# Order within a slot of a fused attention and expert kernel: short products, 1/l and lower parts moved, x's split in quarters

## The chip, the cores and the metric

The kernel runs on one core of one Trainium2 chip. Its engines are TensorE (PE, with its weight loads PEld), VectorE (DVE), ScalarE (ACT), GpSimd (POOL) and SyncE (SP), which only issues transfers here. The metric is the device time of one execution in microseconds (us).

## The reference

Attention with a compressive memory (4 batches, 8 heads, 576 positions, 64 dimensions), and behind it an expert layer over all 2304 tokens:

```python
scores = scale * np.matmul(q, k.transpose(0, 1, 3, 2))        # causal mask
a = np.exp(scores - scores.max(-1, keepdims=True))
a /= a.sum(-1, keepdims=True) + 1e-09
local = np.matmul(a, v)
mem_out = np.einsum('bhsd,bhde->bhse', phi(q), M_prev) / mem_norm
x = g * mem_out + (1 - g) * local                             # g: gate from beta
h = x @ w_in                                                  # 512 -> 2048
out = softplus(h) @ w_out                                     # 2048 -> 512
```

Inputs are wide; the kernel keeps nearly full single precision with products of two parts, an upper and a lower one (high x high, high x low, low x high).

## The kernel before

**Units and slots.** The first part of the program is the attention. A unit is two heads of one batch, 16 units in all. A unit has four slots: slot 0 does the query chunks 0 and 1 of 128 rows, slot 1 chunk 2, slot 2 chunk 3, slot 3 the last half chunk; 64 slots in all, and three more at the end for what is late. In this text units count from 1, slots of a unit from 0, and slots of the whole loop (t in the code) from 0.

**The work of a slot.** `emit_S`: scores on PE into `s` (two buffers), the maximum `nm` on DVE (L357, or L376 in slot 3), `nm` scaled on ACT, and P with its row sums l on ACT (L364, L378). One slot later `emit_split`: r = 1/l on DVE (`rr`, L390 and L393), then the upper half of P times r on POOL (L408, L417) and the lower half on DVE (L409, L419), both into `PHL`; SP's transposing transfers bring them into `PTA` or `PTB`. Three slots after its scores comes `emit_pv`: it turns the memory's part `mem` into the PSUM tile `xp` (L433) and adds P times v (L443); ACT copies the result into `x` (L446). The first part of a unit (A, 256 positions) has its `emit_pv` in slot 3, the second (B, 320 positions) in slot 2 of the next unit.

**Preparation.** For the next unit small steps lie in fixed slots: in slot 2 `v0b` makes v's scale `sc` on DVE from the short PE product `sp`; in slot 3 `f2` makes `ph` (ACT, then DVE, L305); in slot 0 `v2` makes v's lower half; in slot 1 `f3` has the products `np` on PE (L314) and from them `mem` on DVE (L315 to L318, eight operations). `np` uses the PSUM buffers `sm` and `xp`, so the next `emit_pv` comes behind `mem` on PE.

**Expert pieces.** As soon as tokens are complete, four blocks of 384 tokens get a first share of the expert layer while the attention still runs: a piece a slot, six of 12 matmuls (`hp`, one for each of six groups of 128 expert columns, L153) and then four of 18 (`op`, L153). `fill_step` issues a piece; what follows it on other engines (`posts`: Softplus and cast on ACT, the lower part of g on DVE, L91; for `op` the copy `pb` and its transfer) comes in the next slot. Before a block's first piece `split_x` splits x into upper parts (POOL, L99) and lower ones (DVE, L91), four of each. The weights arrive as 64-bit floats; a decode step takes one POOL, three DVE operations (L137 to L141), a cast on ACT and a subtraction on DVE (L91), 12 steps at `WRATE` a slot.

**What sets the order.** In the attention part PE, DVE, ACT and POOL run in the order in which the code issues (a manual schedule); SP's queue is ordered by a scheduler. A slot is issued as: `posts`; `emit_S`; `emit_split` of the slot before; `emit_pv`; the piece; the preparation steps; a decode. After the attention the rest of the expert layer runs under the scheduler, which may also put pieces of it into the last slots.

Of the kernel before, what the change touches and what calls it, by code (L numbers as in the profile page):

```python
# [11 lines left out]
F32R = mybir.dt.float32r  # L12
# [17 lines left out]
GRPS = [6, 10]  # L30
NWB = 6
PVLAG = 3
WRATE = 0.6
GA = GRPS[0]


# [10 lines left out]
def attn_softplus_moe(  # L47
# [28 lines left out]
    x = res.tile([128, NP, NT], F32, name="x")  # L76
# [6 lines left out]
    CAP = 384  # L83
# [6 lines left out]
    def sub(eng, out, in0, in1):  # L90
        eng.tensor_tensor(out=out, in0=in0, in1=in1, op=ALU.subtract)  # L91
# [80 lines left out]
    def emit_g(pool, hp, n, cap, gb):  # L172
        l = pool.tile([128, cap], F32, tag="l", name="l", bufs=3)[:, :n]
        g = pool.tile([128, 2, cap], F32R, tag="g", name="g", bufs=gb)
        A.activation(out=l, in_=hp[:, :n], func=AF.Softplus)  # L175
        cast(A, g[:, 0, :n], l)
        sub(V, g[:, 1, :n], l, g[:, 0, :n])
        return g

    def out_pairs(f, g, dm, n):  # L180
        w = wt[f]
        wh, wl = w[:, 1, 0, dm * 128:(dm + 1) * 128], w[:, 1, 1, dm * 128:(dm + 1) * 128]
        return [(wh, g[:, 0, :n]), (wh, g[:, 1, :n]), (wl, g[:, 0, :n])]

    blocks, work, ready, posts = deque(), deque(), {}, deque()
    XLAG = 2

    def split_x(pool, t0, kd, xt, ea, eb):
        src = x[:, kd, t0:t0 + CAP]
# [3 lines left out]
    def push_fill(k):  # L193
        st = {}
        t0 = k * CAP

        def xs():
            st["x"] = moe1.tile([128, 2, 4, CAP], F32R, tag="xhl", name="xhl", bufs=1)
            for kd in range(4):
                split_x(moe1, t0, kd, st["x"], P, V)  # L200

        def h(f):
            hp = emit_h(moe1, f, st["x"], CAP, CAP)

            def post():
                st[f] = emit_g(moe1, hp, CAP, CAP, GA)
            return post

        def o(dm):
            op = ps_r.tile([128, 512], F32, tag="h", name="op", bufs=2)  # L210
            pairs = []
            for f in range(GA):
                pairs += out_pairs(f, st[f], dm, CAP)
            mm3(op[:, :CAP], pairs, True, True)

            def post():
                pb = moe1.tile([128, CAP], F32, tag="l", name="pb", bufs=3)
                A.copy(pb, op[:, :CAP])
                SY.dma_start(out=part[:, dm, t0:t0 + CAP], in_=pb)
            return post  # L220

        blocks.append((k, xs))
        work.extend([(12, k, h, f) for f in range(GA)] + [(3 * GA, k, o, dm) for dm in range(4)])

    def next_block(t):
        if blocks:
            k, xs = blocks.popleft()
            xs()
            done.add(k)
            ready[k] = t + XLAG  # L230

    def fill_step(t, force=False):

        if not work:
            return
        n, k, fn, j = work[0]
        if k not in done:
            next_block(t)  # L240
        if not force and ready.get(k, 1 << 30) > t:
            return
        work.popleft()
        posts.append(fn(j))
        if n == 12 and j == GA - 1:
            next_block(t)

    def run_posts():
        while posts:
            posts.popleft()()  # L250


    units = [Unit(b, p) for b in range(B) for p in range(NP)]
# [126 lines left out]
            w = 1  # L380
        return pts, l[:, :w]

    def emit_split(u, cs, pts, l):
        r = at.tile([128, 4], F32, tag="rr", name="rr", bufs=3)[:, :l.shape[1]]
        p = u.p
        if cs == (4,):
            ci = cinv4[:, p:p + 1]
        else:
            ci = cinv[:, 2 * p:2 * p + 2].unsqueeze(1).to_broadcast([128, len(cs), 2])
        V.scalar_tensor_tensor(out=r if cs == (4,) else r.rearrange("p (c h) -> p c h", h=2),  # L390
                               in0=l if cs == (4,) else l.rearrange("p (c h) -> p c h", h=2),
                               scalar=1e-9 * ESH, in1=ci, op0=ALU.add, op1=ALU.mult)
        V.reciprocal(out=r, in_=r)  # L393
        w = "A" if cs[0] < 2 else "B"
        if w not in u.pt:
            shape = [128, 8, 256] if w == "A" else [128, 18, 320]
            u.pt[w] = at.tile(shape, F16, tag="PT" + w, name="PT" + w, bufs=2 if w == "B" else 1)
        dst = u.pt[w]
        for j, c in enumerate(cs):
            pt = pts[j]  # L400
            ph = at.tile([128, (c + 1) * 512 if c < 4 else 2 * S], F16, tag=f"PHL{c}", name="PHL", bufs=1)
            if c < 4:
                nk = c + 1
                o = ph.rearrange("p (k t h s) -> p k t h s", t=2, h=2, s=128)
                for h in range(2):
                    rh = r[:, 2 * j + h:2 * j + h + 1]
                    src = pt[:, h * nk * 128:(h + 1) * nk * 128].rearrange("p (k s) -> p k s", s=128)
                    P.tensor_scalar(out=o[:, :, 0, h, :], in0=src, scalar1=rh, scalar2=0.0, op0=ALU.mult, op1=ALU.add)  # L408
                    V.scalar_tensor_tensor(out=o[:, :, 1, h, :], in0=src, scalar=rh, in1=o[:, :, 0, h, :],  # L409
                                           op0=ALU.mult, op1=ALU.subtract)  # L410
                q0 = (c - (0 if w == "A" else 2)) * 128
                SY.dma_start_transpose(out=dst[:, 0:4 * nk, q0:q0 + 128], in_=ph)
            else:
                o = ph[:, 0:1024].rearrange("p (k t s) -> p k t s", t=2, s=128)
                src = pt[:, 0:512].rearrange("p (k s) -> p k s", s=128)
                o4, s4 = ph[:, 1024:1152], pt[:, 512:576]
                P.tensor_scalar(out=o[:, :, 0, :], in0=src, scalar1=r, scalar2=0.0, op0=ALU.mult, op1=ALU.add)  # L417
                P.tensor_scalar(out=o4[:, 0:64], in0=s4, scalar1=r, scalar2=0.0, op0=ALU.mult, op1=ALU.add)
                V.scalar_tensor_tensor(out=o[:, :, 1, :], in0=src, scalar=r, in1=o[:, :, 0, :], op0=ALU.mult,  # L419
                                       op1=ALU.subtract)  # L420
                V.scalar_tensor_tensor(out=o4[:, 64:128], in0=s4, scalar=r, in1=o4[:, 0:64], op0=ALU.mult,
                                       op1=ALU.subtract)
                d = dst.rearrange("p (j h) q -> p j h q", h=2)
                for h in range(2):
                    SY.dma_start_transpose(out=d[:, :, h, 256:320], in_=ph[64 * h:64 * h + 64, 0:1152])
# [51 lines left out]
    with ExitStack():  # L477
# [26 lines left out]
        prev = None  # L504
        wcred = 0.0
        decode = deque()
        t = 0
        while t < ns or late or prev is not None:
            cur = None
            if t < ns:  # L510
                i, c = slots[t]
                u = units[i]
                if c[0] == 0 and i + 1 < len(units):
                    loads(i + 1)
                    plan(i + 1, t)
                run_posts()
                cur = (u, c) + emit_S(u, c)
                if c[0] in (0, 4):
                    late.setdefault(t + PVLAG, []).append((u, "A" if c[0] == 0 else "B"))
            else:  # L520
                run_posts()
            if prev is not None:
                emit_split(*prev)
            for a in late.pop(t, []):
                emit_pv(*a)
            fill_step(t)
            for f in prep.pop(t, []):
                f()
            if decode:
                a, b = decode.popleft()  # L530
                a()
                posts.append(b)
            wcred += WRATE
            while wcred >= 1 and pieces:
                wcred -= 1
                decode.append(pieces.popleft()())
            prev = cur
            t += 1
        run_posts()
        assert not pieces and not prep and not decode  # L540

        order.close()
        attn_ctx.close()
        while work and work[0][1] in done:
            fill_step(t, True)
            run_posts()
        wb = ctx.enter_context(tc.tile_pool(name="wb", bufs=1, side="right", reuse_waits="tile"))
        hcnt.append(0)
        moe2 = ctx.enter_context(tc.tile_pool(name="moe2", bufs=1, reuse_waits="tile"))
# [33 lines left out]
        for i in range(len(seq) + LAG):  # L583
            if i < len(seq):
                s, f = seq[i]
                fl = steps[s][2]
                fi = f - fl[0]
                hp = emit_h(moe2, f, xh[s], CAP, CAP)
                gs[i] = emit_g(moe1, hp, CAP, CAP, GA)
                for _ in range(2 if i % 3 == 0 else 1):  # L590
                    if pieces:
                        pieces.popleft()()
                if fi == 0:
                    if s == len(rest):
                        partial(s)
                    if s + 1 < len(steps):
                        partial(s + 1)
                if s + 1 < len(steps) and 1 <= fi < 5:
                    next_x(s + 1, fi - 1)
# [81 lines left out]
```

## Time and profile before

| | us |
|---|---|
| median of 3 runs | 722.59 (721.75 to 723.76) |
| profiled execution | 720.95 |
| its span, first to last instruction | 719.2 |
| attention part, until about | 410 |

| engine | busy us of the span | share |
|---|---|---|
| PE | 599.6 | 83% |
| DVE | 413.5 | 57% |
| ACT | 313.8 | 44% |
| POOL | 125.9 | 18% |

The shares are means over two parts that differ: after about 410 us PE is the one busy engine, before it PE and DVE take turns. So the rows below are cut by stretches and by slots. Times in a row are the start and the duration; the bracket at a row's end is the idle time of the engine just before it and what ended that.

### The profile page before, as it was taken

Reading aid. Unit: us, or ns where it says so; the run is one execution under the profiler, and the core shown is the slowest. Engines: PE = TensorE matmul, PEld = TensorE weight load, DVE = VectorE, ACT = ScalarE, POOL = GpSimd, SP = SyncE. Lnnn points to the kernel's source line nnn. Section 1 sums busy time; section 2 is a strip of 40 time slices with the busy share of each in tenths; the row PEclk is TensorE's granted clock in tenths of the full one; section 3 lists DMA queues with packets and bytes.
Section 4 is the critical chain, followed back from the end, with each engine's and each line's share of the span. In section 5 each row is a group of like instructions: output and inputs, shape, how many; then the busy total and the mean of one; then the engine's idle time right before and its main releaser. Section 6 shows DMA issues by size and latency. Waiting matters only on the chain.

```text
span 719.2 us, 10758 instructions
## 1 busy us (share of the span) xinstructions
PE 599.6 (83%) x3928; PEld 527.3 (73%) x3928; DVE 413.5 (57%) x918; ACT 313.8 (44%) x797; POOL 125.9 (18%) x218
## 2 busy tenths in 40 slices
PE   6553553847986679989888999999999999999998
PEld 4332332636864557767666899999999999999997
DVE  4788787887578785777678368886203122220211
ACT  6444544357565564665466245444213232321221
POOL 1323223322124231223123112220000000000000
PEclk9566756769997898989999999999999999999999
DMA  5656556435576564644743455571200202010001
GB/s 186 140 123 163 149 111 164 118 72 130 119 160 129 104 128 96 152 91 100 150 85 68 101 173 192 205 226 67 73 16 23 67 0 88 1 45 1 22 23 45
DMA packets 125749, 73.87 MB, mean 103 GB/s; under 512 B 105728, under 2 KB 115456, under 8 KB 125696
## 3 DMA queue, kind: packets, MB, share of 16 engines
q1 hardware_dynamic: 125696, 73.18, 41.2%
q8 instruction: 31, 0.51, 0.3%
q14 instruction: 22, 0.18, 0.1%
HBM read 38.03 MB, written 9.44 MB: 66 GB/s over the span
## 4 chain that ended last, share of the span: by engine, by line
PE 64%; DVE 23%; ACT 5%; issue 3%; POOL 3%; DMA 1%; SPq 0%; ACTq 0%; POOLq 0%
PE hp L153 26%; PE acc L153 21%; DVE PHL L409 7%; PE op L153 7%; PE xp L443 5%; DVE nm L357 4%; DVE mem L318 2%; PE xp L433 2%; ACT P L364 2%; POOL PHL L408 2%; PE s L343 1%; DVE xhl L91 1%; PE s L370 1%; DVE wu L139 1%; DVE wu L141 1%
## 5 line engine op out<-in xcount | busy, mean ns | idle before, releaser
L153 PE MATMUL hp<-xhl,w 128*128 128x384 f32 x1152 | 220.8, 341 | 3.5 <-DVE a L315 3.5
L153 PEld LDWEIGHTS hp<-xhl,w 128*128 128x128 f32 x1152 | 202.4, 189 | 6.1 <-issue 3.7
L153 PE MATMUL acc<-g,w 128*128 128x384 f32 x864 | 161.6, 337 | 0.1
L153 PEld LDWEIGHTS acc<-g,w 128*128 128x128 f32 x864 | 151.7, 188 | 0.6 <-DVE pl L617 0.4
L91 DVE TENSOR_TENSOR g<-l,g 128x384 fp32r<-128x384 f32 x96 | 53.7, 560 | 139.9 <-ACT g L97 139.0
L175 ACT ACTIVATE l<-hp 128x384 f32<-128x384 f32 x96 | 46.9, 490 | 155.3 <-PE hp L153 153.1
L408 POOL TENSOR_SCALAR PHL<-P,rr 128x128 f16<-128x128 f32 (+3 forms) x128 | 67.9, 546 | 233.6 <-ACT nm L360 131.4
L409 DVE SCALAR_TENSOR_TENSOR PHL<-P,rr,PHL 128x128 f16<-128x128 f32 (+3 forms) x128 | 88.5, 739 | 35.4 <-POOL PHL L408 35.4
L343 PE MATMUL s<-kp,mq 64*128 64x128 f32 (+3 forms) x256 | 57.5, 536 | 27.2 <-ACT P L364 16.3
L433 PE MATMUL xp<-identf,mem 128*128 128x128 f32 (+1 forms) x80 | 21.2, 351 | 68.9 <-DVE mem L318 67.2
L433 PEld LDWEIGHTS xp<-identf,mem 128*128 128x128 f32 (+1 forms) x80 | 10.5, 167 | 80.5 <-issue 75.0
L364 ACT ACTIVATE P<-s,nm 128x128 f32<-128x128 f32 (+3 forms) x128 | 66.1, 525 | 4.1 <-ACT nm L360 0.4
L153 PE MATMUL op<-g,w 128*128 128x384 f32 x288 | 54.9, 344 | 1.0 <-DVE g L91 1.0
L357 DVE TENSOR_REDUCE nm<-s 128x2 f32<-128x256 f32 (+1 forms) x64 | 50.9, 816 | 3.7 <-PE s L352 3.7
L443 PEld LDWEIGHTS <-vb 128*64 128x64 f16 x640 | 41.5, 142 | 15.3 <-issue 3.0
L153 PEld LDWEIGHTS op<-g,w 128*128 128x128 f32 x288 | 50.0, 190 | 2.5 <-DVE g L91 1.3
L97 ACT CAST w<-wu 128x512 fp32r<-128x512 f32 x32 | 19.9, 621 | 73.3 <-DVE wu L141 73.3
L360 ACT ACTIVATE nm<-nm 128x2 f32<-128x2 f32 (+1 forms) x48 | 9.8, 204 | 96.3 <-DVE nm L357 96.3
L97 ACT CAST g<-l 128x384 fp32r<-128x384 f32 x96 | 49.2, 513 | 2.6
L343 PEld LDWEIGHTS s<-kp,mq 64*128 64x128 f32 x256 | 21.3, 203 | 37.1 <-ACT P L364 19.0
L443 PE MATMUL xp<-PTB,vb 128*64 128x320 f16 (+2 forms) x448 | 45.0, 378 | 0.0
L137 POOL TENSOR_SCALAR wu<-ws 128x512 f32<-128x512 f32 x32 | 29.3, 915 | 66.9 <-DMA ws<-in_w_in_dram 35.7
(74 smaller groups left out, 583.7 us busy)
## 6 DMA issues: line engine op xcount, KB each, us to landing
ws<-in_w_in_dram SPq DMA_DIRECT2D x16, 512.0 KB, 3.9
ws<-in_w_out_dram SPq DMA_DIRECT2D x16, 512.0 KB, 3.5
mq<-in_nat_dram SPq DMA_DIRECT2D x16, 353.0 KB, 3.4
pl<-part SPq DMA_DIRECT2D x7, 768.0 KB, 5.9
va<-in_nat_dram SPq DMA_DIRECT2D x16, 320.0 KB, 3.2
kp<-in_nat_dram SPq DMA_DIRECT2D x16, 288.0 KB, 3.7
out_dram<-pl SPq DMA_DIRECT2D x24, 192.0 KB, 1.9
part<-pb SPq DMA_DIRECT2D x16, 192.0 KB, 2.1
```

The source lines that it names most:

```text
L91: eng.tensor_tensor(out=out, in0=in0, in1=in1, op=ALU.subtract)
L97: A.copy(out, in_)
L137: P.tensor_scalar(out=tu, in0=sw[:, :, 1], scalar1=RB, scalar2=1.0, op0=ALU.mult, op1=ALU.mult)
L153: nc.tensor.matmul(out, lhsT=l, rhs=r, start=start and i == 0, stop=stop and i == n - 1)
L175: A.activation(out=l, in_=hp[:, :n], func=AF.Softplus)
L343: return mm(s[:, h, o:o + n], lhsT=u.qp[rows[h], c * 128:(c + 1) * 128], rhs=u.kp[rows[h], :n], start=True, stop=True, skip_group_check=True)
L357: V.tensor_reduce(out=nm[:, 2 * j:2 * j + 2], in_=s[:, :, o:o + n], op=ALU.max, axis=AX.X, negate=True)
L364: A.activation(out=pts[j][:, h * n:h * n + n], in_=s[:, h, o:o + n], func=AF.Softplus, scale=SCALE, bias=nm[:, 2 * j + h:2 * j + h + 1], a ...
L408: P.tensor_scalar(out=o[:, :, 0, h, :], in0=src, scalar1=rh, scalar2=0.0, op0=ALU.mult, op1=ALU.add)
L409: V.scalar_tensor_tensor(out=o[:, :, 1, h, :], in0=src, scalar=rh, in1=o[:, :, 0, h, :], op0=ALU.mult, op1=ALU.subtract)
L433: nc.tensor.matmul(xp[:, c * 128 - q0:min(c * 128 + 128, S) - q0], lhsT=u.mem[r, c, :], rhs=identf[r, r], start=c in (0, 2), stop=False, i ...
L443: nc.tensor.matmul(xp[r, lo:n], lhsT=u.vb[:, vi, kc, r], rhs=pt[:, kc * 4 + t * 2 + h, lo:n], start=False, stop=kc == kcs[-1] and i == len ...
```

## The change

- A slot is issued as: `posts`, without the lower part of g, which goes into a queue `los`; 1/l of the slot before (`emit_r`, cut out of `emit_split`); `emit_S`; the split of P of the slot before; `emit_pv`; `los`; the preparation steps; the piece; the due quarters of x's split; a decode.
- x's split of a block is put into a queue `xq`, one quarter (one POOL cast, one DVE subtraction) a slot behind a block's last `hp` piece, two a slot where no block is in work. A block's first piece waits until its quarters are out: all 40 pieces run one slot later, in slots 21 to 30 and 37 to 66 instead of 20 to 29 and 36 to 65.
- `WRATE` goes from 0.6 to 0.5: a decode step every second slot, the last DVE part in slot 24 instead of 21.

```diff
-WRATE = 0.6
+WRATE = 0.5
...
-        sub(V, g[:, 1, :n], l, g[:, 0, :n])
-        return g
+        return g, lambda: sub(V, g[:, 1, :n], l, g[:, 0, :n])
...
-        def xs():
-            st["x"] = moe1.tile([128, 2, 4, CAP], F32R, tag="xhl", name="xhl", bufs=1)
-            for kd in range(4):
-                split_x(moe1, t0, kd, st["x"], P, V)
+        def xs(kd):
+            if kd == 0:
+                st["x"] = moe1.tile([128, 2, 4, CAP], F32R, tag="xhl", name="xhl", bufs=1)
+            split_x(moe1, t0, kd, st["x"], P, V)
...
-    def next_block(t):
+    def next_block(t, step):
         if blocks:
             k, xs = blocks.popleft()
-            xs()
+            xq.extend([(t + 1 + kd // step, lambda kd=kd: xs(kd)) for kd in range(4)])
             done.add(k)
-            ready[k] = t + XLAG
+            ready[k] = t + 1 + 4 // step
...
         while t < ns or late or prev is not None:
-            cur = None
+            cur, rr = None, None
+            run(posts)
+            if prev is not None:
+                rr = emit_r(*prev)
             if t < ns:
...
-                run_posts()
                 cur = (u, c) + emit_S(u, c)
...
             if prev is not None:
-                emit_split(*prev)
+                emit_split(*prev[:3], rr)
             for a in late.pop(t, []):
                 emit_pv(*a)
-            fill_step(t)
+            run(los)
             for f in prep.pop(t, []):
                 f()
+            fill_step(t)
+            split_due(t)
             if decode:
```

On DVE, slot 1 of unit 13 (t = 49) before, from the end of the slot ahead to the first step of `mem`:

```order
L91 TENSOR_TENSOR g<-l,g 128x384
L357 TENSOR_REDUCE nm<-s 128x2
L390 SCALAR_TENSOR_TENSOR rr<-l,cinv 128x4
L393 RECIPROCAL rr<-rr 128x4
L409 SCALAR_TENSOR_TENSOR PHL<-P,rr,PHL 128x128 x2
L409 SCALAR_TENSOR_TENSOR PHL<-P,rr,PHL 128x2x128 x2
L315 TENSOR_SCALAR a<-np 128x6
```

The same slot on DVE after the change (its lines lie a few further down in the file):

```order
L393 SCALAR_TENSOR_TENSOR rr<-l,cinv 128x4
L396 RECIPROCAL rr<-rr 128x4
L360 TENSOR_REDUCE nm<-s 128x2
L415 SCALAR_TENSOR_TENSOR PHL<-P,rr,PHL 128x128 x2
L415 SCALAR_TENSOR_TENSOR PHL<-P,rr,PHL 128x2x128 x2
L91 TENSOR_TENSOR g<-l,g 128x384
L318 TENSOR_SCALAR a<-np 128x6
```

1/l went ahead of the maximum, and the lower part of g from ahead of both to behind the lower halves of P.

On PE, slot 2 of unit 13 (t = 50) before, from the last product of P and v to the next slot's scores:

```order
L443 MATMUL xp<-PTB,vb 64x64
L153 MATMUL hp<-xhl,w_170 128x384 x12
L287 LDWEIGHTS mean
L287 MATMUL sp<-sm,mean 128x1
L287 LDWEIGHTS mean
L287 MATMUL sp<-sm,mean 128x1
L370 MATMUL s<-kp,mq 64x288 x4
```

The same place on PE after the change:

```order
L449 MATMUL xp<-PTB,vb 64x64
L290 LDWEIGHTS mean
L290 MATMUL sp<-sm,mean 128x1
L290 LDWEIGHTS mean
L290 MATMUL sp<-sm,mean 128x1
L153 MATMUL hp<-xhl,w_169 128x384 x12
L373 MATMUL s<-kp,mq 64x288 x4
```

The short product `sp` went ahead of the piece (which is the one of the group before, since pieces start a slot later); `np` in slot 1 did the same.

On DVE, unit 11, slot 1 (t = 41) before, where the third block's x is split between the lower halves of P and `mem`:

```order
L409 SCALAR_TENSOR_TENSOR PHL<-P,rr,PHL 128x128 x2
L409 SCALAR_TENSOR_TENSOR PHL<-P,rr,PHL 128x2x128 x2
L91 TENSOR_TENSOR xhl<-x,xhl 128x384 x4
L315 TENSOR_SCALAR a<-np 128x6
L316 RECIPROCAL a<-a 128x6
```

After the change the quarters of this block's split end four slots (t = 43 to 46); the third of them, in slot 1 of unit 12, on DVE:

```order
L321 TENSOR_TENSOR mem<-np,a 128x256
L91 TENSOR_TENSOR xhl<-x,xhl 128x384
L393 SCALAR_TENSOR_TENSOR rr<-l,cinv 128x2
L396 RECIPROCAL rr<-rr 128x2
L360 TENSOR_REDUCE nm<-s 128x2
```

The four subtractions left the place ahead of `mem`; one stands behind it, at the slot's end.

## Rows read from the trace of the kernel before

**Rows 1.** Stretches: us; busy us of PE, PEld, DVE, ACT, POOL; clock; DMA

```profile
12.06:145.09 133.03, 70.76 (x504) 45.89 (x500) 106.45 (x236) 61.60 (x171) 38.69 (x63) 0.67 0.57 135
...
234.58:410.00 175.42, 149.08 (x1084) 121.04 (x1085) 121.44 (x295) 96.83 (x267) 43.77 (x80) 0.91 0.52 108
86.96:113.13 26.17, 11.29 (x89) 6.62 (x89) 20.40 (x47) 12.37 (x34) 7.16 (x12) 0.63 0.53 139
286.03:307.76 21.73, 21.04 (x165) 17.54 (x166) 16.11 (x40) 13.77 (x38) 5.21 (x10) 1.00 0.63 143
410.00:719.20 309.20, 305.71 (x1764) 303.82 (x1762) 113.20 (x204) 96.98 (x202) 17.53 (x20) 1.00 0.23 75
```

**Rows 2.** Waits until 410 us: who waited for whom, us, times, longest

```profile
PE xp L433 <- DVE mem L318: 67.2, 14, 8.3
...
DVE PHL L409 <- POOL PHL L408: 35.4, 48, 0.9
...
DVE sc L288 <- PE sp L287: 25.4, 10, 4.3
...
DVE PHL L419 <- POOL PHL L417: 14.5, 16, 1.2
```

**Rows 3.** Timeline of DVE, slot 2 of unit 8: start, us, instruction

```profile
204.63 1.22 DVE L357 TENSOR_REDUCE nm<-s 128x2 f32<-128x1024 f32 x1
...
206.90 1.46 DVE L409 SCALAR_TENSOR_TENSOR PHL<-P,rr,PHL 128x384 f16<-128x384 f32 x2 [0.78 <-POOL PHL L408]
```

**Rows 4.** Timeline of POOL, the same slot: the two upper halves

```profile
206.27 1.15 POOL L408 TENSOR_SCALAR PHL<-P,rr 128x384 f16<-128x384 f32 x2 [4.62 <-ACT nm L360]
```

**Rows 5.** Timeline of DVE, a decode step in slot 0 of unit 5

```profile
116.01 0.66 DVE L421 SCALAR_TENSOR_TENSOR PHL<-P,rr,PHL 128x64 f16<-128x64 f32 x1
...
117.39 0.41 DVE L138 TENSOR_SCALAR wu<-wu 128x512 int32<-128x512 int32 x1
...
119.94 0.69 DVE L91 TENSOR_TENSOR w<-wu,w 128x512 fp32r<-128x512 f32 x1 [0.68 <-ACT w L97]
```

**Rows 6.** Timeline of DVE, unit 13: the maxima and three other operations

```profile
307.76 1.02 DVE L357 TENSOR_REDUCE nm<-s 128x2 f32<-128x256 f32 x2
...
310.65 0.27 DVE L421 SCALAR_TENSOR_TENSOR PHL<-P,rr,PHL 128x64 f16<-128x64 f32 x1
...
318.41 1.22 DVE L357 TENSOR_REDUCE nm<-s 128x2 f32<-128x1024 f32 x1
...
325.58 0.16 DVE L288 TENSOR_SCALAR sc<-sp 128x1 int32<-128x1 int32 x1 [3.44 <-PE sp L287]
...
327.05 0.75 DVE L376 TENSOR_REDUCE nm<-s 128x1 f32<-128x576 f32 x1
...
331.00 2.87 DVE L91 TENSOR_TENSOR xhl<-x,xhl 128x384 fp32r<-128x384 f32 x4
...
334.94 1.01 DVE L357 TENSOR_REDUCE nm<-s 128x2 f32<-128x256 f32 x2
```

**Rows 7.** Timeline of PE, unit 13: np, start of slot 2's P·V, a piece

```profile
312.16 1.28 PE L314 MATMUL np<-mq,ph 128*128 128x130 f32 x10
...
318.18 0.96 PE L433 MATMUL xp<-identf,mem 128*128 128x128 f32 x3 [3.57 <-DVE mem L318]
...
327.58 2.36 PE L153 MATMUL hp<-xhl,w 128*128 128x384 f32 x12
```

**Rows 8.** Timeline of PE, unit 8: the scores of slot 3

```profile
207.19 1.19 PE L370 MATMUL s<-kp,mq 64*64 64x288 f32 x8
```

**Rows 9.** Stretches of slot 2's P·V in units 8 and 13, columns as rows 1

```profile
204.86:207.13 2.27, 2.27 (x33) 1.79 (x33) 1.46 (x4) 1.17 (x4) 0.86 (x2) 1.00 0.39 114
318.18:322.26 4.08, 4.08 (x32) 2.82 (x32) 3.15 (x6) 1.65 (x5) 1.15 (x2) 0.50 0.20 36
```

**Rows 10.** Timeline of ACT: slot 2's last row sum, slot 3's part of ph

```profile
207.41 0.20 ACT L364 ACTIVATION_READ_ACCUMULATOR P<-s,nm 128x1 f32 x1
...
329.21 0.68 ACT L304 ACTIVATE ph<-mq 128x576 f32<-128x576 f32 x1
```

More of the change, by code (lines that the diff above doesn't have):

```diff
@@ L183, in out_pairs @@
         return [(wh, g[:, 0, :n]), (wh, g[:, 1, :n]), (wl, g[:, 0, :n])]
-    blocks, work, ready, posts = deque(), deque(), {}, deque()
-    XLAG = 2
+    blocks, work, ready, posts, los, xq = deque(), deque(), {}, deque(), deque(), deque()
     def split_x(pool, t0, kd, xt, ea, eb):
@@ L205, in post @@
             def post():
-                st[f] = emit_g(moe1, hp, CAP, CAP, GA)
+                st[f], lo = emit_g(moe1, hp, CAP, CAP, GA)
+                los.append(lo)
             return post
@@ L239, in fill_step @@
         if k not in done:
-            next_block(t)
+            next_block(t, 2)
         if not force and ready.get(k, 1 << 30) > t:
@@ L245, in fill_step, with split_due, run @@
         if n == 12 and j == GA - 1:
[L246 to L250, printed above, removed]
+            next_block(t, 1)
+    def split_due(t):
+        while xq and xq[0][0] <= t:
+            xq.popleft()[1]()
+    def run(q):
+        while q:
+            q.popleft()()
     units = [Unit(b, p) for b in range(B) for p in range(NP)]
@@ L381, in emit_S, with emit_r @@
         return pts, l[:, :w]
-    def emit_split(u, cs, pts, l):
+    def emit_r(u, cs, pts, l):
         r = at.tile([128, 4], F32, tag="rr", name="rr", bufs=3)[:, :l.shape[1]]
@@ L393, in emit_split @@
         V.reciprocal(out=r, in_=r)
+        return r
+    def emit_split(u, cs, pts, r):
         w = "A" if cs[0] < 2 else "B"
@@ L519, in attn_softplus_moe @@
                     late.setdefault(t + PVLAG, []).append((u, "A" if c[0] == 0 else "B"))
-            else:
-                run_posts()
             if prev is not None:
-                emit_split(*prev)
+                emit_split(*prev[:3], rr)
             for a in late.pop(t, []):
                 emit_pv(*a)
-            fill_step(t)
+            run(los)
             for f in prep.pop(t, []):
                 f()
+            fill_step(t)
+            split_due(t)
             if decode:
@@ L538, in attn_softplus_moe @@
             t += 1
-        run_posts()
+        run(posts)
+        run(los)
+        split_due(t + 9)
         assert not pieces and not prep and not decode
@@ L545, in attn_softplus_moe @@
             fill_step(t, True)
-            run_posts()
+            run(posts)
+            run(los)
+            split_due(t + 9)
         wb = ctx.enter_context(tc.tile_pool(name="wb", bufs=1, side="right", reuse_waits="tile"))
@@ L588, in attn_softplus_moe @@
                 hp = emit_h(moe2, f, xh[s], CAP, CAP)
-                gs[i] = emit_g(moe1, hp, CAP, CAP, GA)
+                gs[i], lo = emit_g(moe1, hp, CAP, CAP, GA)
+                lo()
                 for _ in range(2 if i % 3 == 0 else 1):
```

## The prediction

> **What bounds the kernel now.** I read the stretches first [rows 1]. After 410 us TensorE is busy 305.71 of 309.20 us at full clock, and the change leaves the order of that part as it is, so only the 410 us before can move. I cut them at starts of units: stretch A (units 1 to 5, 12 to 145 us) has hardly any expert pieces and eleven of the twelve weight decodes; stretch B (units 6 to 9, to 234.58) has one decode and ten expert pieces; stretch C (units 10 to 16, to 410 us) has thirty pieces. In A VectorE is busy 106.45 of 133.03 us and TensorE, at clock 0.67, 70.76. In C TensorE is busy 149.08 of 175.42 and VectorE 121.44. Nothing is full: what sets the time is who hands over to whom inside a slot. Unit 12 shows the contrary, TensorE busy 21.04 of 21.73 us at clock 1.00; there is nothing to win in it [rows 1].
>
> The waits come next [rows 2]. Before 410 us VectorE stands idle 35.4 + 14.5 us for GpSimd's upper half of P (48 and 16 times: 0.74 and 0.91 us each) and 25.4 us for the short product sp; TensorE stands idle 67.2 us for mem, which VectorE writes. The last two form a ring in each unit: mem (slot 1) releases the P·V product of slot 2, behind which stand the expert piece, sp and the scores of slot 3; sp and those scores release VectorE, which makes the next mem.
>
> **1/l ahead of the maximum.** In one slot 2 the maximum took 1.22 us, then came 1/l, and only then GpSimd's two upper halves, 1.15 us; VectorE stood 0.78 us and went on with the lower ones, 1.46 us [rows 3, 4]. In the new order 1/l is out first and GpSimd works under the maximum (0.75 to 1.22 us by slot [rows 3, 6]). A unit has three waits of 0.74 and one of 0.91: at most 3.1 us. I don't count all of it. In slot 2 of a unit without pieces sp lies behind a P·V product of 4.08 us at half clock [rows 9], while VectorE now arrives after 1.22 + 0.33 (1/l, two short operations) + 1.46 = 3.0 us: it waits for sp instead, and slot 2's 0.74 is gone. In slot 3 VectorE goes on to ph, which needs ScalarE's part: that ended at 329.89, 2.84 us after the maximum's start [rows 6, 10]; VectorE would now be there after some 2.4 us: 0.4 is lost. And 1/l itself can now wait for l. In slot 2 l was there 1.76 us after the maximum's end (205.85 to 207.61 [rows 3, 10]); slot 0 has two more row sums to read, an estimate of 2.1 us, against about 1.8 us of VectorE work before 1/l: 0.3. That leaves 3.1 - 0.74 - 0.4 - 0.3, about 1.6 us a unit; the ends are 0 and 3.1. A: 5 x 1.6 = **8.0**. B: 4 x 1.6 = **6.4**.
>
> **The slower decode rate.** One decode holds VectorE from 117.39 to 120.63, 3.24 us, with 0.68 of it waiting for ScalarE's cast, and a small operation beside GpSimd's part took 0.66 instead of 0.27 us: 3.6 in all [rows 5, 6]. Unit 4 (two decodes) is 26.17, so a bare unit is 19.0 [rows 1]. At 0.5 a slot nine decodes stay in A and three fall into B: A gains 2 x 3.6 = **7.2**, B pays **7.2**. If expert pieces hide them in B, up to 7 us more is won; I count none, since VectorE is the later engine in units with decodes.
>
> **x's split in quarters.** Now four subtractions stand in one lump of 2.87 us, once for each of four blocks [rows 6]; in one of them the lump stands ahead of mem. After the change block 0's split lies half in A, half in B (A gains **1.4**, B pays it), block 1's half in B, half in C (B gains 1.4, C pays **1.4**). Blocks 2 and 3 get a quarter (0.72) at the end of each slot that carries an 18-matmul piece, where TensorE is the later engine by more than that: both lumps go, **5.7** in C. GpSimd's casts move with them, behind its upper halves. If that cover failed the 5.7 would come back.
>
> **Short products ahead of the piece, lower part of g later.** Take unit 13, four 12-matmul pieces: 307.76 to 334.94 [rows 6].
> - Slots 0 and 1 take 10.65; less 0.91 + 0.74 for GpSimd, 9.0.
> - Slot 2 takes 8.64. TensorE waited 3.57 us for mem, the clock fell to 0.50 and the P·V product took 4.08 us; in unit 8 the same product at clock 1.00 took 2.27 [rows 7, 9]. With np ahead of the piece, TensorE in slot 1 still has np (1.28), the piece (2.36, 2.3 to the next start) and the next scores (1.2, as those of slot 3) to do while VectorE makes mem [rows 7, 8]: 4.8 against the 5.4 or so that slot 1 has of the 9.0 above. The wait shrinks to some 0.5 to 1 us, like the 0.69 idle of unit 12, which kept its clock [rows 1]. Then 2.27 + 0.2 (sp) + 2.3 (piece) + 1.2 (scores) = 6.0 from the product's start at 318.18 to the next maximum, 5.7 from the maximum at 318.41 [rows 6 to 8]: 2.9 less, 1.8 of it from the clock, the rest because sc and g's lower part no longer stand between sp and the maximum.
> - Slot 3 takes 7.89; without the lump (2.87) and GpSimd's wait it is 4.1, and TensorE's P·V (14 matmuls, an estimate of 1.0 by the 33 in 2.27 us [rows 9]), piece (2.3) and scores (1.1) want 4.4, which decides.
>
> Unit 13 becomes 19.1 instead of 27.2. For all of C: slot 2 in six units (not in 12), at 2.2 each, between the clock's 1.8 alone and 2.9: **13.2**. Slots 0, 1 and 3: about four and a half units' worth of 12-matmul slots; a piece of 18 keeps TensorE the later one, so I take **6.0** where 4.5 x 1.65 would be 7.4. The tail: pieces start one slot later, so one more 18-matmul piece stands after the last slot, behind the last P·V: **-3.3**, by 18 times a twelfth of the piece's 2.36 (3.5) [rows 7], less what overlaps.
>
> **The sum.** A: 8.0 + 7.2 + 1.4 = 16.6. B: 6.4 - 7.2 - 1.4 + 1.4 = -0.8. C: 13.2 + 6.0 + 5.7 - 1.4 - 3.3 = 20.2. Together 36.0. The profiled execution took 720.95 us (span 719.2); the median of the three runs is 722.59, 1.6 above it. 722.6 - 36.0 = **686.6**.
>
> **Rivals.**
> - The clock stays low. If TensorE still waits over 2 us for mem, because g's lower part and nothing else of weight now stands before mem, each slot 2 keeps its half clock and C's 13.2 is gone: 722.6 - 22.8 = 699.8. For it: g's 0.5 us does move ahead of mem. Against it: the lump and the GpSimd wait ahead of mem both go. 0.18.
> - GpSimd collides. Its decode step and the x casts now run right behind the upper halves, just when the lower ones want to run. The row shows 0.39 us lost beside GpSimd's part [rows 5, 6]. At the worst a lower half waits for a whole GpSimd operation: by the 0.57 of an upper half of 384 numbers [rows 4] an estimate of 0.6 for a cast of as many and 0.8 for a decode's 512. 16 x 0.6 and 12 x (0.8 - 0.4, which the row pays already) are 14.4: 701. 0.08. The Trainium skill (SBUF — State Buffer, Who interferes with whom) says that a VectorE instruction with two SBUF inputs contends with a GpSimd instruction that reads SBUF, and that a reduction never does; by that the maximum is the right thing to put beside GpSimd and the lower halves the wrong one, which would make this rival's 701; the trace agrees so far as the 0.66 against 0.27 goes.
> - Slower: 1/l blocks VectorE's queue. 1/l of slot t now stands ahead of the maximum of t + 1, behind it the whole queue, and ScalarE's next row sums wait for that maximum. It decides once l comes later than VectorE's own work by more than 36.0 / 64 = 0.56 us in every slot; ScalarE would have to be held up by the piece's Softplus and cast ahead of nm. At 1.0 us in each slot: 686.6 + 64 = 750. Against it: l came 1.76 us after the maximum, and slots last 4 to 8 us. 0.03.
> - The waits only change their name: VectorE's 50 us turn into waits for TensorE, and the lumps and the decode shift alone remain, 1.4 + 5.7 - 1.4 and the tail: 720. 0.03.
>
> **How the numbers follow.** The forecast, 676 to 697, gets 0.68; between its rivals and below 676 the rest. Its low end: all 3.1 us a unit in A and B would give 9 x 1.5 = 13.5 more, of which I let 10 in. The high end of the range takes in the clock rival and part of GpSimd's: 676 to 704. A difference of 0.3% (2 us) is what a measurement of this kernel can tell from none. Faster 0.94, same 0.03, slower 0.03.
>
> **What would show it.** VectorE's idle time for PHL from GpSimd near zero; the wait of TensorE for mem under 25 us instead of 67.2; a granted clock of C near 1.00 and its length near 155 us; stretch A near 116; unit 13 near 19. A new wait of 1/l for ScalarE's row sums over 20 us, or lower halves of P longer than now, would prove me wrong; so would a second part longer than 309 us.

## The result and the profile after

The changed kernel takes 681.1 us (median of 4 runs, 678.99 to 683.53) against 722.2 in the same measurement: a ratio of 0.943, 95% interval 0.9392 to 0.9467. Faster was right, 681.1 lies inside the range of 676 to 704, and the gain is 41.1 us where 36.0 was forecast. The profiled execution took 678.99 (span 677.2, 42.0 shorter than before).

First the stretches of the kernel after, cut at the same first maxima as in [rows 1]: A, B, C with the tail, then units 4, 12 and 13, then the second part (columns as there: us; busy us of PE, PEld, DVE, ACT, POOL; clock; DMA).

```profile
10.95:125.42 114.47, 64.52 (x469) 41.43 (x470) 96.49 (x228) 60.64 (x169) 36.35 (x59) 0.69 0.63 150
125.42:216.97 91.55, 73.37 (x546) 55.71 (x546) 69.40 (x175) 53.60 (x147) 27.13 (x47) 0.84 0.61 129
216.97:372.00 155.03, 147.39 (x1136) 120.12 (x1136) 113.80 (x299) 98.47 (x272) 43.69 (x82) 0.97 0.60 128
76.77:100.34 23.57, 12.33 (x100) 8.36 (x100) 19.84 (x47) 12.36 (x34) 7.22 (x12) 0.72 0.66 156
259.22:280.29 21.07, 21.07 (x166) 17.39 (x167) 15.43 (x42) 13.25 (x37) 5.99 (x13) 1.00 0.64 150
280.29:299.36 19.07, 17.98 (x148) 14.25 (x149) 15.51 (x43) 14.61 (x41) 5.45 (x11) 1.00 0.67 139
372.00:677.20 305.20, 300.97 (x1717) 299.96 (x1715) 112.25 (x200) 95.04 (x197) 15.26 (x20) 1.00 0.22 72
```

A went from 133.03 to 114.47, B from 89.49 to 91.55, unit 13 from 27.18 to 19.07 with its clock from 0.87 to 1.00; unit 12, which TensorE fills, shrank by 0.66 only. Units 10 to 15 went from 146.91 to 122.53. The first addition of a partial sum in the second part, an operation that both traces have, moved from 510.54 to 468.56 us: 42.0, the whole gain, lies ahead of it (1.1 of it ahead of A, which begins at 10.95 instead of 12.06).

The waits until 375 us (engine, tile and line, releaser; us in total, times, longest), VectorE's and then one of TensorE's; they answer to [rows 2].

```profile
DVE nm L379 <- PE s L376: 20.9, 9, 3.4
DVE sc L291 <- PE sp L290: 14.3, 9, 3.1
...
DVE nm L360 <- PE s L355: 9.4, 12, 1.5
...
DVE PHL L415 <- POOL PHL L414: 3.8, 14, 0.3
DVE rr L393 <- ACT P L367: 2.2, 4, 1.2
```

```profile
PE xp L439 <- DVE rr L393: 46.2, 11, 7.0
```

GpSimd's 35.4 us are 3.8, sp's 25.4 are 14.3, and VectorE now waits 30.3 us for scores. Before these were 9.8: 3.7 for L357, shown below, and the rest in slot 3:

```profile
DVE nm L376 <- PE s L373: 6.1, 4, 5.1
```

TensorE's wait for mem is 46.2 instead of 67.2; the releaser named is the operation that follows mem on VectorE.

The lower halves of P and the maxima by line (shape of one form, count, busy us, mean ns, idle before), after and then before: VectorE's own work in the 128 lower halves fell by 13.5 us.

```profile
L415 DVE SCALAR_TENSOR_TENSOR PHL<-P,rr,PHL 128x128 f16<-128x128 f32 (+3 forms) x128 | 75.0, 630 | 3.8 <-POOL PHL L414 3.8
L360 DVE TENSOR_REDUCE nm<-s 128x2 f32<-128x256 f32 (+1 forms) x64 | 50.4, 809 | 9.4 <-PE s L355 9.4
```

```profile
L409 DVE SCALAR_TENSOR_TENSOR PHL<-P,rr,PHL 128x128 f16<-128x128 f32 (+3 forms) x128 | 88.5, 739 | 35.4 <-POOL PHL L408 35.4
L357 DVE TENSOR_REDUCE nm<-s 128x2 f32<-128x256 f32 (+1 forms) x64 | 50.9, 816 | 3.7 <-PE s L352 3.7
```

And slots 1 and 2 of unit 13 (start, duration), the place of [rows 7]: on TensorE np, the piece, the P·V product after an idle time of 1.09 us instead of 3.57, at full clock (2.4 GHz; half, as before the change, is 1.2); then slot 2's lower halves on VectorE.

```profile
283.41 1.38 PE L317 MATMUL np<-mq,ph 128*128 128x130 f32 x10
284.55 2.33 PE L153 MATMUL hp<-xhl,w 128*128 128x384 f32 x12
...
289.14 0.61 PE L439 MATMUL xp<-identf,mem 128*128 128x128 f32 x3 [1.09 <-DVE rr L393]
289.69 1.72 PE L449 MATMUL xp<-PTB,vb 128*64 128x320 f16 x28
```

```profile
290.30 1.19 DVE L415 SCALAR_TENSOR_TENSOR PHL<-P,rr,PHL 128x384 f16<-128x384 f32 x2
```

### The profile page after: what moved, and what is told of

The parts are those of the page before. It is cut to its first block, busy times and chain, and to the rows that moved or that the text cites. A ratio compares the mean times of both kernels' runs of the same rounds, so it can differ in the third digit from the quotient of the medians.

```text
span 677.2 us, 10759 instructions
## 1 busy us (share of the span) xinstructions
PE 593.0 (88%) x3928; PEld 523.0 (77%) x3928; DVE 395.9 (58%) x918; ACT 314.1 (46%) x797; POOL 123.7 (18%) x218
## 5 line engine op out<-in xcount | busy, mean ns | idle before, releaser
L415 DVE SCALAR_TENSOR_TENSOR PHL<-P,rr,PHL 128x128 f16<-128x128 f32 (+3 forms) x128 | 75.0, 630 | 3.8 <-POOL PHL L414 3.8
L439 PE MATMUL xp<-identf,mem 128*128 128x128 f32 (+1 forms) x80 | 19.9, 332 | 46.3 <-DVE rr L393 46.2
L449 PEld LDWEIGHTS <-vb 128*64 128x64 f16 x640 | 37.8, 131 | 12.0 <-issue 2.9
L137 POOL TENSOR_SCALAR wu<-ws 128x512 f32<-128x512 f32 x32 | 27.6, 862 | 72.8 <-DMA ws<-in_w_in_dram 25.5
L91 DVE TENSOR_TENSOR xhl<-x,xhl 128x384 fp32r<-128x384 f32 x48 | 25.3, 571 | 25.7 <-ACT xhl L97 25.6
```

The lines of the kernel that those rows point to most:

```text
L137: P.tensor_scalar(out=tu, in0=sw[:, :, 1], scalar1=RB, scalar2=1.0, op0=ALU.mult, op1=ALU.mult)
L439: nc.tensor.matmul(xp[:, c * 128 - q0:min(c * 128 + 128, S) - q0], lhsT=u.mem[r, c, :], rhs=identf[r, r], start=c in (0, 2), stop=False, i ...
L449: nc.tensor.matmul(xp[r, lo:n], lhsT=u.vb[:, vi, kc, r], rhs=pt[:, kc * 4 + t * 2 + h, lo:n], start=False, stop=kc == kcs[-1] and i == len ...
```

## The experiments

Five kernels are the changed one with one part undone (the decode rate of 0.6 is one of them), two are the kernel before with one or two parts alone, and four more, told below the table, add multiplications to a changed kernel or take the decode rate to 0.7. The stretches are distances of first maxima in each profiled execution; C here is units 10 to 15. The kernel before took 721.2, 721.6 and 721.1 us in the three measurements.

| kernel | us | against before [95% interval] | A | B | C |
|---|---|---|---|---|---|
| before | 722.2 | | 133.0 | 89.5 | 146.9 |
| changed | 681.1 | 0.943 | 114.5 | 91.6 | 122.5 |
| changed, 1/l behind the maximum | 719.7 | 0.9975 [0.9957, 0.9993] | 124.8 | 98.1 | 140.9 |
| changed, lower part of g first | 697.9 | 0.968 [0.966, 0.970] | 115.1 | 91.2 | 136.8 |
| changed, x's split in a lump | 685.2 | 0.950 [0.948, 0.952] | 116.3 | 90.0 | 128.6 |
| changed, piece ahead of short products | 685.0 | 0.950 [0.947, 0.952] | 115.2 | 94.4 | 123.3 |
| changed, rate 0.6 | 676.3 | 0.938 [0.936, 0.940] | 120.3 | 81.2 | 122.7 |
| before, 1/l first | 704.7 | 0.977 [0.974, 0.979] | 121.0 | 85.2 | 141.0 |
| before, 1/l first and g's part late | 685.5 | 0.951 [0.949, 0.953] | 120.9 | 79.7 | 135.2 |

**1/l behind the maximum again.**

```diff
-            if prev is not None:
-                rr = emit_r(*prev)
...
-                emit_split(*prev[:3], rr)
+                emit_split(*prev[:3], emit_r(*prev))
```

> The changed kernel with one part undone: 1/l stands behind the maximum again, the rest as in the change. Theory (the parts add up, each by its own hand-over): the terms of the prediction come back, 8.0 in stretch A, 6.4 in B and about 6 in C, so 681.1 + 20 = 701 (697 to 705); VectorE's idle time for PHL from GpSimd is near 50 us again and the clock of stretch C stays above 0.94. Rival 1 (the clock does it): with GpSimd's wait back ahead of mem TensorE loses its clock in C, which falls below 0.93, and some 13 us more go: 710 to 716. Rival 2 (waits only change their name, since VectorE waits 30 us for the scores in the changed kernel): under 10 us, 683 to 691.

Measured 719.7: all but 1.4 us of the change is gone with this one edit, more than the theory (697 to 705) and both rivals said. A and B lose 10.3 and 6.5, near the terms of 8.0 and 6.4; C loses 18.3 instead of 6, and 5.9 more go behind unit 16's first maximum. Its waits until 400 us, and unit 13 on VectorE and then TensorE, read as in the kernel before:

```profile
DVE PHL L415 <- POOL PHL L414: 35.1, 47, 0.9
...
DVE PHL L425 <- POOL PHL L423: 13.3, 15, 0.9
```

```profile
318.94 1.46 DVE L415 SCALAR_TENSOR_TENSOR PHL<-P,rr,PHL 128x384 f16<-128x384 f32 x2 [0.78 <-POOL PHL L414]
```

```profile
316.91 0.95 PE L439 MATMUL xp<-identf,mem 128*128 128x128 f32 x3 [2.97 <-DVE mem L321]
317.79 3.20 PE L449 MATMUL xp<-PTB,vb 128*64 128x320 f16 x28
```

np stands ahead of the piece here, g's lower part stands late, and the lump is gone. TensorE waits 2.97 us for mem all the same and the product runs at half clock. Here the order on TensorE frees nothing; VectorE makes mem as late as before: the transposes that wait for mem start 10.74 us after unit 13's first maximum, 10.42 before the change, 8.85 in the changed kernel.

**Lower part of g ahead of 1/l again.**

```diff
-                los.append(lo)
+                lo()
```

> The changed kernel with one part undone: the lower part of g stands ahead of 1/l and the maximum again, 24 times. Theory (it takes a quarter to a half of its 0.5 us in the slots where VectorE is the later engine): 682 to 686, clock of C unchanged. Rival 1 (it waits for ScalarE's cast and 1/l and the maximum with it, so TensorE waits for mem and the clock falls): 688 to 695 with the clock of C at 0.94 or lower. Rival 2 (TensorE's pieces hide it): 680 to 682.

Measured 697.9: 16.8 us for the place of 24 operations of 0.56, which run either way. The theory falls and the first rival's mechanism holds, with C's clock at 0.93 and the time 2.9 above its range: VectorE runs ahead of ScalarE now, reaches g's part before the cast that it reads has ended (1.25 us ahead of slot 1's maximum in unit 13), and 1/l, the maximum and mem stand behind it. The same operations stand at this place before the change, with 2.0 us of such waits in all: there VectorE mostly came after the cast had ended. Unit 13 on VectorE, the group of waits until 400 us here and until 410 before, and TensorE:

```profile
289.12 0.56 DVE L91 TENSOR_TENSOR g<-l,g 128x384 fp32r<-128x384 f32 x1 [1.25 <-ACT g L97]
```

```profile
DVE g L91 <- ACT g L97: 25.4, 17, 3.0
```

```profile
DVE g L91 <- ACT g L97: 2.0, 5, 1.2
```

```profile
294.89 0.61 PE L439 MATMUL xp<-identf,mem 128*128 128x128 f32 x3 [2.89 <-DVE mem L321]
295.43 2.88 PE L449 MATMUL xp<-PTB,vb 128*64 128x320 f16 x28
```

**The same, with TensorE kept at work.** Is that loss the clock, or VectorE's wait? Ahead of the P·V product of each slot 2:

```diff
+            if t < ns and late.get(t, [(0, 0)])[0][1] == "B":
+                hp = ps_r.tile([128, 512], F32, tag="h", name="hp", bufs=2)
+                for _ in range(12):
+                    nc.tensor.matmul(hp[:, :256], lhsT=ident, rhs=id2.rearrange("p i n -> p (i n)"), start=True, stop=True)
```

> The kernel with the lower part of g ahead of 1/l again (697.9 us), and twelve multiplications of constants, 256 columns each, whose result nobody reads, ahead of the P.V product of every slot 2, where TensorE is idle for mem. They shorten nothing on VectorE and only keep TensorE at work. Theory 1 (the lost 16.8 us are mostly the clock that falls while TensorE waits for mem): the product runs in 1.72 us in stretch C, the clock of C is 0.98 or more and the time comes down to 684 to 690. Theory 2 (they are VectorE's waits for ScalarE's cast of g, on the chain to mem and to the next maximum, and the clock follows from them): the clock rises, the time stays at 694 to 699. Between, 690 to 694: both, with the parts read from the difference.

Measured 694.1 (0.963 of before, 0.960 to 0.966), 3.8 of the 16.8 given back. In unit 13 the product is back at full clock:

```profile
291.30 1.48 PE L533 MATMUL hp<-id,ident 128*128 128x256 bf16 x12
294.25 0.61 PE L439 MATMUL xp<-identf,mem 128*128 128x128 f32 x3 [1.47 <-DVE mem L321]
294.79 1.72 PE L449 MATMUL xp<-PTB,vb 128*64 128x320 f16 x28
```

The product is 1.16 us shorter, the unit 0.80 (22.23 for 23.03; 19.07 without g's part ahead). So of unit 13's loss of 3.96 the clock holds 0.8 and VectorE's order the rest. The sum over the kernel is less clean: in units 11 and 14 the product still took 2.9 and 3.0 us, unit 12, which TensorE fills, grew by 1.2, and of the 5.2 us between the two profiled executions 3.6 lie behind unit 16's first maximum, where that unit's product went from half to full clock. The second theory holds, at its lower edge.

**The piece ahead of the short products again.**

```diff
             run(los)
+            fill_step(t)
             for f in prep.pop(t, []):
                 f()
-            fill_step(t)
```

> The changed kernel with one part undone: the expert piece stands ahead of the short products np and sp again, the rest as in the change (lower part of g behind P, x's split in quarters, 1/l first). Theory (the short products ahead of the piece carry stretch C's slot 2): TensorE waits over 2 us for mem in slot 2 of the units with pieces, the clock of C falls to 0.93 or lower, and most of the 13.2 us of the prediction's slot 2 comes back, with sp late besides: 690 to 697. Rival (what freed mem was VectorE's side, the lump and GpSimd's wait): TensorE has np early enough either way, C keeps its clock at 0.96 or more, 681 to 685.

Measured 685.0: the rival. In unit 13 the piece now comes first and np 2.2 us later, mem comes as it did in the changed kernel, and the unit takes 19.06 instead of 19.07. TensorE's wait there is 1.08 us (1.09), and C's clock 0.99:

```profile
286.39 2.38 PE L153 MATMUL hp<-xhl,w 128*128 128x384 f32 x12
288.61 1.28 PE L317 MATMUL np<-mq,ph 128*128 128x130 f32 x10
...
292.14 0.61 PE L439 MATMUL xp<-identf,mem 128*128 128x128 f32 x3 [1.08 <-DVE rr L393]
```

VectorE needs np only behind its lower halves and g's part, 290 us in this unit, when np had just ended. What the edit costs, 2.9 us in B, 0.7 in A and C each, goes with sp, as far as the waits tell: VectorE's wait for it until 400 us is 36.5 us instead of 14.3.

**x's split in one lump again**, the pieces in the slots that they have.

```diff
-            xq.extend([(t + 1 + kd // step, lambda kd=kd: xs(kd)) for kd in range(4)])
+            xq.extend([(t, lambda kd=kd: xs(kd)) for kd in range(4)])
```

> The changed kernel with one part undone: the four quarters of x's split stand in one lump again, at the end of the slot in which the block before gave its last 12-matmul piece; the pieces stay in the slots they have. Theory (each part its own price): two lumps of 2.87 us in stretch C come back on the path, 5.7 us, the other two lie in no piece's way: 686 to 688, the clock of C within 0.02 of the changed kernel's 0.97. Rival 1 (the clock does it): a lump ahead of mem lets TensorE wait and its clock fall in C, 690 to 695. Rival 2 (the pieces of 18 matmuls hide a lump as well as quarters): 680 to 682.

Measured 685.2, 4.1 lost where 5.7 was the price, within the interval's 1.5 us of the theory's lower end; C is 6.1 longer. Not by the theory's route, though. Unit 14 alone lost 6.0, and VectorE and then TensorE show how:

```profile
303.90 2.87 DVE L91 TENSOR_TENSOR xhl<-x,xhl 128x384 fp32r<-128x384 f32 x4 [0.40 <-POOL xhl L99]
...
309.74 0.54 DVE L91 TENSOR_TENSOR g<-l,g 128x384 fp32r<-128x384 f32 x1
```

```profile
310.33 0.62 PE L153 MATMUL op<-g,w 128*128 128x384 f32 x2 [2.69 <-DVE g L91]
...
312.46 0.95 PE L439 MATMUL xp<-identf,mem 128*128 128x128 f32 x3 [0.30 <-DVE rr L393]
313.34 3.20 PE L449 MATMUL xp<-PTB,vb 128*64 128x320 f16 x28
```

The lump pushes the lower part of the block's last g back, the first 18-matmul piece waits 2.69 us for it with two matmuls to go, and the P·V product behind runs at half clock. The lump of the block before cost unit 11 2.2 us, and unit 10, without its quarters, won as much.

**The kernel before with 1/l first, and with g's part late besides.** The edits are those of the change: `emit_r` cut out and placed ahead of `emit_S`; then `los`, run ahead of the piece.

> The kernel before with one part of the change alone: 1/l ahead of the maximum; decode rate, lumps of x, lower part of g and the piece ahead of the short products stay as before. Theory after the first four runs (one chain on VectorE, from 1/l to mem, sets TensorE's wait ahead of the P.V product of slot 2, and the clock holds once that wait is about 1 us and not at 3): stretches A and B gain some 16 us, C little, since g's lower part still stands on that chain and now waits for ScalarE: 702 to 710, wait of 2.5 us or more in unit 13, clock of C at 0.94 or lower. Rival (the parts add up as their undoing priced them, 38 us for 1/l): 681 to 687.

> The kernel before with two parts of the change alone: 1/l ahead of the maximum, and the lower part of g behind P; decode rate, lumps of x and the piece ahead of the short products stay as before. Theory (the chain from 1/l to mem): these two are nearly the whole change; what is missing is what undoing the other two cost, 4 and 4 us: 686 to 692, the wait in unit 13 near 1 us, the clock of C 0.96 or more. Rival (the short products ahead of the piece and the quarters are needed for it too): 698 or more, the clock of C at 0.94 or lower.

Measured 704.7, as the theory said, and 685.5, half a us under its 686 to 692: 1/l alone brings 16.9 us, g's part 19.2 more: 36.1 by the two, where the whole change brings 41.1. Unit 13's P·V product on TensorE in the first and in the second:

```profile
300.73 0.96 PE L436 MATMUL xp<-identf,mem 128*128 128x128 f32 x3 [3.36 <-DVE mem L318]
```

```profile
289.88 0.61 PE L440 MATMUL xp<-identf,mem 128*128 128x128 f32 x3 [1.07 <-DVE rr L394]
```

One miss: the second kernel's clock in units 10 to 15 is 0.92, not the 0.96 expected: in units 10 and 11 TensorE still waits 3.81 and 4.11 us for mem. The quarters and the short products together mend that (the kernel at rate 0.6 below has both: 2.06 and 1.10). The kernels at rate 0.5 tell them apart: with both these waits are 2.42 and 0.93 us, with the quarters alone 0.84 and 1.08, with the short products alone 3.83 and 0.95. So in unit 10 it is the quarters; in unit 11 either does.

**The decode rate back at 0.6, and at 0.7.**

> The changed kernel with one part undone: the decode rate is 0.6 a slot again. Theory (a decode costs VectorE 3.6 us wherever it lies): stretch A 6 to 8 us longer, B as much shorter, together within 2 of the changed kernel: 679 to 683. Rival 1 (expert pieces hide decodes in B, so moving them there was a gain): 685 to 689, B shorter by under 4 us. Rival 2 (decodes beside pieces cost more): 675 to 678.

> The changed kernel with the decode rate at 0.7 a slot instead of 0.5, so that all twelve decodes lie ahead of the first expert pieces. Theory (a decode costs 2.9 us in stretch A and 5.2 in B, as the rate of 0.6 showed): one more decode moves, 673 to 676. Rival 1 (decodes closer than two slots collide on ScalarE and in the two buffers of the loaded weights): 677 to 681. Rival 2 (the gain at 0.6 was that of one particular pair of slots in units 6 and 7): 675.5 to 678.

Measured 676.3 and 676.4 (0.938, 0.935 to 0.941): in both the second rival holds. The slower rate of the change is a loss of 4.8 us, and past 0.6 nothing more is to be had. The stretches A, B and C of the kernel at 0.6:

```profile
11.80:132.06 120.26, 66.32 (x487) 41.67 (x482) 101.97 (x235) 61.43 (x171) 37.75 (x61) 0.68 0.64 150
132.06:213.21 81.15, 68.50 (x533) 51.62 (x534) 63.31 (x167) 51.93 (x145) 25.20 (x45) 0.87 0.66 135
213.21:335.88 122.67, 116.25 (x904) 92.63 (x904) 94.85 (x254) 83.42 (x230) 37.62 (x71) 0.96 0.63 133
```

Two decodes moved back from B to A. A grew by 5.8, 2.9 for one; B shrank by 10.4, 5.2 for one, nearly all of it in units 6 and 7 (26.59 and 24.99 at 0.5, 21.50 and 20.12 at 0.6). In unit 6 of the changed kernel, decode and piece wait for each other. ScalarE waits 0.91 us for the piece, makes its Softplus and cast and only then the decode's cast, for which VectorE waits 1.67 us; TensorE waits 4.81 us for mem, ahead of which VectorE had another decode to do (130.03 to 133.27). The decode's subtraction on VectorE, ScalarE and then TensorE:

```profile
147.01 0.69 DVE L91 TENSOR_TENSOR w<-wu,w 128x512 fp32r<-128x512 f32 x1 [1.67 <-ACT w L97]
```

```profile
145.42 0.49 ACT L175 ACTIVATE l<-hp 128x384 f32<-128x384 f32 x1 [0.91 <-PE hp L153]
...
146.36 0.62 ACT L97 CAST w<-wu 128x512 fp32r<-128x512 f32 x1
```

```profile
138.48 0.95 PE L439 MATMUL xp<-identf,mem 128*128 128x128 f32 x3 [4.81 <-DVE rr L393]
139.37 3.20 PE L449 MATMUL xp<-PTB,vb 128*64 128x320 f16 x28
```

At 0.6 TensorE's wait is 1.90 us and the transposes run at full clock.

**TensorE kept at work where no piece is.** Does the half clock limit stretch A? To the changed kernel the twelve multiplications were added ahead of each P·V product without an open piece (condition `t in late and t < ns and not work`); then, at rate 0.7, 32 of them in A and 12 in unit 9, ahead of slot 2's product alone.

> The changed kernel with something added: in slots that have a P.V product while no expert piece is open, twelve multiplications of constants, 256 columns each, whose result nobody reads, stand ahead of the P.V product, where TensorE is idle for up to 7 us. Theory (in units without pieces the P.V product at half clock holds up sp, for which VectorE waits 1.5 to 3 us in slot 2): with the clock up the product takes 2.3 us instead of 4.2, and five to seven units gain 1 to 1.8 us each: 670 to 677, the product in stretch A under 3 us. Rival 1 (the clock does not rise on so little, or VectorE is the later engine anyway): 679 to 683. Rival 2 (the multiplications themselves lie ahead of the P.V product in slots where it is ready): 684 to 695.

> The changed kernel with the decode rate at 0.7, and ahead of the P.V product of slot 2, in units without an open piece, 32 multiplications of constants of 256 columns in stretch A and 12 behind it, whose result nobody reads; twelve in stretch A had ended 3.5 to 5.8 us before mem came, and the product still took 3.20 us at half clock. Theory (in A sp behind the slow product is what VectorE waits 1.5 us for): the product takes 1.72 us, units 2 to 5 gain 1 to 1.5 us each, 666 to 671. Rival 1 (VectorE is the later engine in A all the same, since behind sp it meets the next wait): as the rate alone or 3 less, 671 to 676. Rival 2 (the multiplications run past mem and hold the product up): 677 or more.

The first took 677.7 us (0.940, 0.938 to 0.942), between the theory's range and the first rival's. A is unchanged (115.0 for 114.5), since twelve end too early: in unit 4 TensorE stands 3.45 us behind them and the product runs at half clock as before. The 3.4 us come from units 9 and 10 (2.4 and 1.3). The second took 670.9 (0.930, 0.928 to 0.932), 5.5 under the rate alone. Unit 4 in the first, unit 5 in the second:

```profile
82.79 2.74 PE L533 MATMUL hp<-id,ident 128*128 128x256 bf16 x12
88.98 0.96 PE L439 MATMUL xp<-identf,mem 128*128 128x128 f32 x3 [3.45 <-DVE rr L393]
89.87 3.20 PE L449 MATMUL xp<-PTB,vb 128*64 128x320 f16 x28
```

```profile
113.43 5.48 PE L533 MATMUL hp<-id,ident 128*128 128x256 bf16 x32
119.63 0.62 PE L439 MATMUL xp<-identf,mem 128*128 128x128 f32 x3 [0.71 <-DVE rr L393]
120.18 1.72 PE L449 MATMUL xp<-PTB,vb 128*64 128x320 f16 x28
```

The product now starts at full clock in units 2 to 5, but only unit 5 became shorter, by 1.5 us; units 3 and 4 stay at 25.8 and 26.0, where they are without. So VectorE is the later engine in most of A. The time is at the border of the theory's 666 to 671 and the first rival's 671 to 676; by the units the rival is right for three of four, and the gain is unit 5's, unit 9's (2.0) and unit 10's (1.2). This kernel is the fastest here, 10 us under the changed one and 50 under the kernel before.

## Why the prediction was right, and where it was not

**The hand-over from GpSimd** was the right centre, and its size for A and B was right: 8.0 and 6.4 predicted, 10.3 and 6.5 by undoing it. That is 2.1 us a unit in A and 1.6 in B, within the bound of 3.1; but in C units 11 and 13 lose 5.3 and 4.9 by the undoing. The bound counted VectorE's waits alone. The lower halves themselves became shorter, 13.5 us over 16 units or 0.8 a unit, since they run beside GpSimd's upper halves for 23.5 us in all instead of 42.4 (42.2 with 1/l behind the maximum; the two of 384 numbers in slot 2 of unit 13 took 1.46 us there, 1.19 after the change). And in C the hand-over also sets when mem comes, a price that the prediction gave to other terms.

**C's 20.2 came out as 24.4, by another route.** (From unit 16's first maximum to the common addition nothing changed: 129.05 and 129.06 us.) The step that failed is slot 2's 13.2 us, put down to np ahead of the piece and to the clock. With np behind the piece unit 13 is 19.06 us all the same. What moves it is 1/l and g's lower part. Counted from unit 13's first maximum, the transposes behind mem start at 8.85 us and TensorE's work ahead of them ends at 7.8; with 1/l undone these are 10.74 and 7.8, with g's part ahead again 9.77 and 6.9, with the piece ahead of np 8.88 and 7.8. So in this unit 1/l and g's part both bring mem earlier, g's part also lets TensorE's own work fill more of the time until then, and np's place does neither. The clock was a smaller part: of the 3.96 us that unit 13 loses with g's part ahead, keeping TensorE at work gave back 0.8. Unit 13's slots came out at 8.9 (0 and 1), 5.8 and 4.4, where 9.0, 5.7 and 4.4 had been worked out. For slot 2 the reason given was another, so that its size fits is luck: a sum that fits says little of its cause.

**Lower part of g: no term of its own, 16.8 measured by undoing it.** The prediction gave it a share of the 1.1 us in slot 2 that it did not put down to the clock, and spoke of its 0.5 us on the way to mem. The change itself makes most of its price: a faster VectorE runs into ScalarE's cast. The rival of the low clock, 699.8 us if TensorE still waits over 2 us, describes that kernel (697.9, wait 2.89), but named g's part as what would cause it from its new place, where it does no harm.

**The decode rate: +7.2 -7.2 was wrong by 4.8.** A decode costs 2.9 in A and 5.2 in B. The prediction saw one possible error, that pieces hide decodes, and left out the other, that decodes hold up pieces.

**x's split** was priced near (5.7; C 6.1, the whole 4.1), but the loss came through g and the 18-matmul piece instead of the lump's own length, so that is luck too. **The tail:** from the last maximum to the common addition it took 108.74 us before and 114.21 after, 5.5 lost where 3.3 was counted for pieces one slot later. That reason is not borne out: with 1/l first alone, where the pieces keep their old slots, it took 113.20, and with g's part late besides 111.88. What lengthens it is not shown.

**The rivals.** Lower halves collide with GpSimd: the reverse, 739 to 630 ns. 1/l blocks VectorE's queue: `rr` waits 2.2 us, four times. Waits that only change their name: in part, 9.8 to 30.3 us for scores, 20.2 of it in C, where TensorE has become the later engine at these places. Of the signs, TensorE's wait for mem under 25 us was wrong: 46.2, of which 40.7 lies in A and B (7.03 in unit 4), where the last runs show that little hangs on it. The other signs came true: C's clock 0.97, A 114.5, unit 13 19.1, and VectorE's wait for slots 0 to 2 of GpSimd's part 3.8.

**The parts do not add up.** Each price is a difference of medians from different measurements, between which the kernel before moved by 1.1 us. Undone one by one they price at 38.6 (1/l), 16.8 (g), 4.1 (x), 3.9 (short products) and -4.8 (rate), 58.6 in all for a change of 41.1. Put on in a row they give 16.9 (1/l), 19.2 (g), 9.2 (x, short products and the pieces a slot later together) and -4.8. Without 1/l all the others are worth 1.4.

## What to carry to other kernels

When two engines hand work to each other in every step, start with the hand-over whose waits stand on the later engine, and then look at what that engine will reach too early: an operation that waited for nobody can become the next bound, and has to move with it. Judge a part both by undoing it in the whole and by doing it alone, since the two prices differ when one part only pays behind another. Put side work such as decoding where the busier partner is not yet at work, even if that engine looks full there.

## What the runs showed of the hardware

A maximum beside GpSimd's upper halves costs what it did without them (816 ns on the mean before, 809 after, 64 times), while lower halves beside them cost more: of the two of 384 numbers before [rows 3, 4] the first, 0.53 us of it beside GpSimd's second upper half, took 0.93 us, and the second, alone, 0.61. The Trainium skill (SBUF — State Buffer, Who interferes with whom) says that a VectorE operation with two SBUF inputs contends with a GpSimd operation that reads SBUF, and that a reduction does not; both halves of it agree with these numbers, though the price here, 0.33 us for 0.53 side by side, is a fraction of an operation and not a wait for a whole one.

TensorE's granted clock, by these rows: in unit 13 a product behind an idle time of 2.89 us began at full clock (transposes 0.61) and fell while it ran (2.88 for 1.72); behind 2.97 us it was at half from its start (0.95, 3.20); behind 1.09 and 1.47 it kept full. The idle time just ahead does not settle it: at rate 0.7 the transposes of unit 6 took 0.61 us behind 3.25 us, at rate 0.6 those of unit 10 0.96 behind 2.06. The other way round, twelve multiplications took 1.48 us at full clock and 2.74 at half; 32 of them took 5.48 us in unit 5, so the clock rose while they ran, and the product behind them was at full.
